# Adaptive LayerNorm with grouped-query attention and a gated MLP: the first eight units' side work in another order, and the last branch marked for prefetch

## The chip, the cores and the metric

The kernel runs on one core of one Trainium2 chip. The metric is the device time of one execution in microseconds (us); a kernel's time is the median of several executions. One further execution is taken by the hardware profiler, and all views of the profile come from that one.

## The reference

`x` is 2048 tokens of 512. There are 32 query heads that share 8 key/value heads of width 128, each with 2048 cached keys. Everything is bfloat16.

```python
mod = (_silu(c) @ w_mod).reshape(...)          # c is 1 x 512, w_mod is 512 x 3072
sa, ca, ga, sb, cb, gb = ...                   # six rows of 512
h = _layernorm(x) * (1 + ca) + sa
x = x + ga * attention(h)                      # q = h @ wq; softmax(q k / sqrt(128)) v; @ wo
h = _layernorm(x) * (1 + cb) + sb
z = gelu(h @ w_in)                             # halves z1, z2 of 896
g = w_sp @ _layernorm(z2) + b_sp
x = x + gb * ((z1 * g) @ w_out)
```

The sum over the 512 rows of `w_mod` may be taken in any order, as long as `c` is taken in the same one.

## The kernel before, in words

**The fast path and the general path.** The kernel computes softmax without subtracting the maximum. It keeps the reciprocals of all softmax sums (`rall`), and checks late in the run that all lie within a safe range; the result is one integer, `flag` (`check_flag`, written in the third stage below). At the very end every engine loads `flag` from on-chip memory into a register (L1360), and `tc.If(redo != 0)` (L1361) runs `general_path`, a whole second kernel that is safe for any input, if the flag is set. On these inputs it is not set, so the program goes past that code. The argument `preferred_fallthrough_block=False` asks that the code for the flag not being set be laid out right behind the branch. L1391 is the end of the whole program, where all engines meet and semaphores are cleared.

**Units and slots.** Attention is a row of 128 units: unit u is key/value head g = u // 16 and the 128 tokens of tile j = u % 16, with its four query heads side by side, so that a score matmul has 512 columns. A unit has 8 slots. In slot i, `qk(u, i)` makes two score matmuls (L922) into a two-bank PSUM tile `s_ps` (two buffers) and one exponential on ScalarE of 128x1024 (L929, `ACTIVATE pT<-s_ps`); `pv(u - 1, i)` makes eight matmuls with the exponentials of the unit before (L944), into `o_ps` (two buffers), and ends every fourth slot with a reciprocal and a scaling on VectorE (L955, L956). So 8 exponentials on ScalarE mark one unit.

**The order by hand.** The schedule is manual: each engine runs its instructions in the order in which the program emits them. Within a slot the loop emits first the entries that `at(unit, slot, fn)` put into `later`, then `qk`, then `pv`, then the entries of `fill`, then (in slots 4 to 7) one matmul of the output projection `wo_proj` (L976) for the unit three back. An instruction on VectorE can therefore hold back everything that was emitted for VectorE after it.

**The side work of the first units.**
- `ln1_stats` (L691, L692 on VectorE, then L672 and L676 on GpSimd) makes mean and reciprocal deviation of up to four token tiles; `ln1_norm` (L680, VectorE) normalises them into `xn`. For the tokens of chunk 0 (512 tokens, of which the first tile is done ahead of everything) and chunk 1, `ln1_turn` (L833) transposes `xn` on TensorE into `misc` (two buffers) and applies scale and shift (L815, VectorE) into `hT`. For chunks 2 and 3, `ln1_dma` (L855) issues four transposing DMAs on SyncE's queue, and `ln1_dma_mod` (L815) applies scale and shift once they have landed.
- `qproj(b, ...)` makes 16 query-projection matmuls (L885), four for each of four heads, into `misc`, and one copy to `qT` on VectorE for each head (L894). Block b serves units 4b to 4b + 3. For block 0 it is done in two parts: 16 small matmuls for the first tile ahead of unit 0, and 16 of 384 columns (`rest_q`) in unit 0, which unit 1 needs.
- `ln1_at(ch, stats, norm, turn)` sets the slots of the three steps of chunk ch. Before: chunk 1 at (0, 7), (1, 3), (1, 6); chunk 2 at (1, 7), (2, 2), (3, 5); chunk 3 at (4, 1), (4, 5), (5, 5). Where the third step is a DMA, it is issued one slot after the second.
- `set_fill(b)`: before, block 1's 16 matmuls are one in each slot of units 2 and 3, and those of block b > 1 one in each of slots 0 to 3 of the four units before block b.
- GpSimd's queue carries, among the reciprocal deviations, four large loads: `wmod_b` (L1083, at (2, 5)), `win_sb` (L1084, at (5, 5)), and `v`, `wo` and `wq` of head 1 (L714, L724, L706, at (5, 3), (6, 3) and (7, 3)). A load waits for its buffer and for its place in that queue, and for nothing else. SyncE's queue carries the transposing DMAs and the load of head 1's keys (L729, at (4, 3)).

**The start.** `c_bf` (L696), one tile of `x` (L697), the first 1024 columns of `w_mod` (`wmod_a`, L698), keys and values are loaded on SyncE's queue. Meanwhile `warm(18)` (L766) runs 18 matmuls on zeros. `mod_columns` (L782) makes scale and shift from `wmod_a`, and the chain through L833, L815, L885 and L894 leads to the first score matmul.

**After attention** come the MLP's first half (L1119, L1158) and four chunks of `spatial` (L1273), each with its output projection (L1294) and the stores to `out` (L1311). The last store is in two halves, one issued by SyncE and one by ScalarE.

Of the kernel before, what the change touches and what calls it, by code (L numbers as in the profile page):

```python
# [15 lines left out]
P = 128  # L16
# [559 lines left out]
def kernel(  # L576
# [23 lines left out]
    REP = HQ // HKV  # L600
# [5 lines left out]
    NDT = D // P  # L606
# [3 lines left out]
    CT = 512 // P  # L610
# [12 lines left out]
    HK = SK // 2  # L623
    k_rows = A_k_cache[0, 0, 0:HK].rearrange("(p t) d -> p t d", p=P)
    v_rows = A_v_cache[0, 0, 0:HK].rearrange("(p t) d -> p t d", p=P)
    wmod_dram = w_mod.rearrange("(dt p) n -> p dt n", p=P)
    c_dram = c[0].rearrange("(j p) -> p j", p=P)
    win_dram = B_w_in.rearrange("(dt p) f -> p dt f", p=P)
    wout_dram = B_w_out.rearrange("(ft p) d -> p ft d", p=P)

# [32 lines left out]
    def bank(name):  # L663
        return psum.tile([P, 512], FP32, name=name)

    def bank2():
        return psum.tile([P, 1024], FP32, name="s_ps")
# [93 lines left out]

    def warm(n):

        w_ps = bank2()
        for k in range(n):
            nc.tensor.matmul(  # L766
                w_ps[:, 0:512].rearrange("p (r d) -> p r d", r=REP),
                lhsT=zeros[:, 0, :],
                rhs=zeros[:],
                start=True,  # L770
                stop=True,
            )
# [23 lines left out]
    def ln1_stats(j0, n):  # L796
        for j in range(j0, j0 + n):
            ln_stats(mv1, j, x_sb[:, j, :])
        return rstd_of(mv1[:, j0 : j0 + n, :], n, "ln1")

    def ln1_norm(j0, n, rstd):
        xns = []
        for j in range(j0, j0 + n):
            xn = res.tile([P, D], BF16, name="xn1", bufs=4)
            normalise(xn[:], x_sb[:, j, :], mv1[:, j, 0:1], rstd[:, j - j0 : j - j0 + 1])
            xns.append(xn)
        return xns

    def hT_of(ch):
        if ch not in hTs:  # L810
            hTs[ch] = res.tile([P, NDT, 512], BF16, name="hT", bufs=NCH)
        return hTs[ch]

    def ln1_mod(dst, src, dt):
        nc.vector.tensor_scalar(  # L815
            out=dst,
            in0=src,
            scalar1=modc[:, NDT + dt : NDT + dt + 1],
            scalar2=modc[:, dt : dt + 1],
            op0=ALU.mult,  # L820
            op1=ALU.add,
        )

    def ln1_turn(j0, n, xns, on_act=()):

        ch, c0 = j0 // CT, (j0 % CT) * P
        hT = hT_of(ch)
        for half in range(2):
            t_ps = bank("misc")[:].bitcast(BF16).rearrange("p (k q) -> p k q", k=2)
            for k in range(2):  # L830
                dt = half * 2 + k
                for jj in range(n):
                    nc.tensor.transpose(  # L833
                        t_ps[:, k, jj * P : (jj + 1) * P],
                        xns[jj][:, dt * P : (dt + 1) * P],
                        ident[:],
                    )
            for k in range(2):
                dt = half * 2 + k
                dst, src = hT[:, dt, c0 : c0 + n * P], t_ps[:, k, 0 : n * P]  # L840
                if dt in on_act:
                    nc.scalar.activation(
                        out=dst,
                        in_=src,
                        func=ACT.Identity,
                        scale=modc[:, NDT + dt : NDT + dt + 1],
                        bias=modc[:, dt : dt + 1],
                    )
                else:
                    ln1_mod(dst, src, dt)  # L850

    def ln1_dma(j0, n, xns):
        hT = hT_of(j0 // CT)
        for jj in range(n):
            nc.sync.dma_start_transpose(out=hT[:, :, jj * P : (jj + 1) * P], in_=xns[jj][:])  # L855

    def ln1_dma_mod(ch):
        for dt in range(NDT):
            ln1_mod(hTs[ch][:, dt, :], hTs[ch][:, dt, :], dt)

    warm(18)
    xns0 = ln1_norm(0, 1, ln1_stats(0, 1))
    mod_columns(0, wmod_a, 0)
# [9 lines left out]
    def qproj(b, heads, c0, n):  # L873

        g, ch = divmod(b, NCH)
        if b not in qTs:
            qTs[b] = early.tile([P, REP, 512], BF16, name="qT")
        one = n * len(heads) <= 512
        ps = {}

        def mm(hh, dt):
            if dt == 0 and (not one or hh == heads[0]):
                ps[0] = bank("misc")
            o0 = (hh - heads[0]) * n if one else 0
            nc.tensor.matmul(  # L885
                ps[0][:, o0 : o0 + n],
                lhsT=wqs[g][:, dt, hh * DH : (hh + 1) * DH],
                rhs=hTs[ch][:, dt, c0 : c0 + n],
                start=(dt == 0),
                stop=(dt == NDT - 1),  # L890
            )
            if dt == NDT - 1 and (not one or hh == heads[-1]):
                hs = heads if one else [hh]
                nc.vector.tensor_copy(  # L894
                    out=qTs[b][:, hs[0] : hs[-1] + 1, c0 : c0 + n],
                    in_=ps[0][:, 0 : len(hs) * n].rearrange("p (h q) -> p h q", q=n),
                )

        return [lambda hh=hh, dt=dt: mm(hh, dt) for hh in heads for dt in range(NDT)]
# [3 lines left out]
    rest0 = {}  # L903
# [7 lines left out]
    def at(it, slot, fn):  # L911
        later.setdefault((it, slot), []).append(fn)
# [142 lines left out]
    def load_wsp(tile_, t, st):  # L1055
        nc.sync.dma_start_transpose(  # L1056
            out=tile_[:, st, :],
            in_=B_w_sp[t * 512 : (t + 1) * 512, st * P : (st + 1) * P],
        )
# [2 lines left out]

    fill = {}
    rest_q = qproj(0, list(range(REP)), P, 512 - P)
    at(0, 3, lambda: ln1_turn(1, CT - 1, rest0["xn"]))
    for k, fn in enumerate(rest_q):
        fill.setdefault((0, 5 + min(k // 5, 2)), []).append(fn)

    def ln1_at(ch, stats, norm, turn):
        st = {}  # L1070
        at(*stats, lambda: st.update(r=ln1_stats(ch * CT, CT)))
        at(*norm, lambda: st.update(x=ln1_norm(ch * CT, CT, st["r"])))
        if ch == 1:
            at(*turn, lambda: ln1_turn(ch * CT, CT, st["x"]))
        else:
            at(norm[0], norm[1] + 1, lambda: ln1_dma(ch * CT, CT, st["x"]))
            at(*turn, lambda: ln1_dma_mod(ch))

    ln1_at(1, (0, 7), (1, 3), (1, 6))
    ln1_at(2, (1, 7), (2, 2), (3, 5))  # L1080
    ln1_at(3, (4, 1), (4, 5), (5, 5))
    rest_w = {}
    at(2, 5, lambda: nc.gpsimd.dma_start(out=wmod_b, in_=wmod_dram[:, :, 2 * D : NMOD]))  # L1083
    at(5, 5, lambda: nc.gpsimd.dma_start(out=win_sb[:], in_=win_dram))  # L1084
# [5 lines left out]
    def set_fill(b):  # L1090

        fs = qproj(b, list(range(REP)), 0, 512)
        for k, fn in enumerate(fs):
            it, slot = ((b - 1) * CT + k // NDT, k % NDT) if b > 1 else (2 + k // 8, k % 8)
            fill.setdefault((it, slot), []).append(fn)

    def wsp0():
# [5 lines left out]
    for g in range(1, HKV):  # L1103
        it = (g - 1) * NT + 4
# [91 lines left out]
    for it in range(NU + 6):  # L1196
        if it < NU:
            if it % CT == 0 and it // CT + 1 < NB:
                set_fill(it // CT + 1)
        elif it == NU:  # L1200
            free_a.close()
            z2p = fast.enter_context(tc.tile_pool(name="z2p", bufs=1))
            zs["z2"] = z2p.tile([P, NT, FH], BF16, name="z2")
# [54 lines left out]
    def check_flag():  # L1258
        f_ps = bank("o_ps")
        nc.tensor.matmul(  # L1260
            f_ps[0:1, 0:1], lhsT=bad[:], rhs=ones_bf[:, 0:1], start=True, stop=True
        )
        nc.vector.tensor_copy(out=flag[:], in_=f_ps[0:1, 0:1])
# [51 lines left out]
    def o2_tile(t, jj):  # L1315
        o2 = bank("o_ps")
        for f in range(NFT):
            o2_mm(o2[:], yTs[t], jj, f)
        finish_tile(t, jj, o2)
# [3 lines left out]
    for t in range(NCH):  # L1323
        yTs[t] = mlp.tile([P, NFT, 512], BF16, name="yT", bufs=2)
        if t == last:
            break
        for f in range(NFT):
            spatial(t, yTs[t], f, 0, 512)
            if t == 1 and f == CT:
                check_flag()  # L1330
            if t > 0 and f < CT:
                o2_tile(t - 1, f)
        if t == 0:
            wsp[last] = wspp.tile([P, NT, 512], BF16, name="wsp")
            for st in range(NT):
                load_wsp(wsp[last], last, st)
    acc = [bank2(), bank2()]
    o2_last = [acc[jj // 2][:, (jj % 2) * 512 : (jj % 2 + 1) * 512] for jj in range(CT)]
    yT = yTs[last]
# [18 lines left out]
    fast.close()  # L1358

    redo = nc.values_load(flag[0:1, 0:1], min_val=0, max_val=P)  # L1360
    with tc.If(redo != 0, preferred_fallthrough_block=False):  # L1361
        general_path(
            tc, A_x, A_k_cache, A_v_cache, A_wq, A_wo, B_x, B_w_in, B_w_sp, B_b_sp, B_w_out,
            c, w_mod, out,
        )
# [30 lines left out]
```

## Time and profile before

| what | us |
|---|---|
| median of 3 runs | 1338.97 (1338.56 to 1339.24) |
| the profiled execution, its own time | 1339.45 |
| its span, first to last instruction | 1337.6 |
| TensorE busy in the span | 1305.1 |
| ScalarE busy in the span | 1079.3 |
| first exponential of unit 0 | 12.40 |
| first exponential of unit 1 | 27.62 |
| first exponential of unit 2 | 37.32 |
| first exponential of unit 4 | 57.02 |
| first exponential of unit 8 | 92.93 |
| last instruction on the data, an output's store, is issued | 1329.39 |

The mean granted TensorE clock over the span is 0.995. In the views, PE is TensorE's matmuls, PEld its weight loads, DVE VectorE, ACT ScalarE, POOL GpSimd, SP SyncE; a q behind the name means the sequencer of that engine. A line of the timeline has its start, its length from first start to last end, the engine, the source line, the operation and its tiles, and in brackets the idle time ahead of it and what ended it.

### The profile page before, as it was taken

How to read it: one execution, taken by the hardware profiler on the slowest of the kernel's cores; microseconds unless marked ns; L12 is line 12 of the kernel's file. 1: busy time of each engine (PE TensorE's matmuls, PEld its weight loads, DVE VectorE, ACT ScalarE, POOL GpSimd, SP SyncE). 2: the span in 40 equal slices, each digit the busy share in tenths (PEclk: the TensorE clock that was granted, in tenths of full speed). 3: DMA queues.
4: the chain of work that ended last, by engine and by line, in shares of the span. 5: the costliest groups of instructions: out<-in, count | busy, mean ns of one | idle time of the engine just before them, and what ended most of it. 6: DMA issues, size and time to landing. Idle time of an engine off the chain costs nothing.

```text
span 1337.6 us, 27647 instructions
## 1 busy us (share of the span) xinstructions
PE 1305.1 (98%) x12126; PEld 859.4 (64%) x12333; DVE 473.1 (35%) x1163; ACT 1079.3 (81%) x1060; POOL 48.6 (4%) x90
## 2 busy tenths in 40 slices
PE   7999999999999999999999999999999999999996
PEld 3666666666666666666666666666666667644444
DVE  4632222222222222222222222222222566783443
ACT  4898999999999999999999999999999999650000
POOL 1200000000000000000000000000000000020000
PEclk8999999999999999999999999999999999999999
DMA  5541022101311121012110310122101111154200
GB/s 158 131 111 17 14 63 37 21 17 33 64 21 21 33 64 21 17 36 65 17 21 17 74 30 14 21 65 36 21 13 21 25 33 33 29 123 82 55 21 27
DMA packets 146368, 57.59 MB, mean 43 GB/s; under 512 B 136544, under 2 KB 141792, under 8 KB 146240
## 3 DMA queue, kind: packets, MB, share of 16 engines
q1 hardware_dynamic: 141888, 39.29, 15.7%
q0 software_dynamic: 4208, 16.39, 4.1%
q8 instruction: 98, 1.61, 0.5%
q14 instruction: 30, 0.25, 0.1%
q10 hardware_dynamic: 144, 0.07, 0.0%
HBM read 21.37 MB, written 2.10 MB: 18 GB/s over the span
## 4 chain that ended last, share of the span: by engine, by line
PE 94%; SPq 2%; DVE 1%; issue 1%; DMA 1%; POOL 0%; ACT 0%; DVEq 0%
PE s_ps L922 35%; PE o_ps L944 35%; PE misc L885 7%; PE misc L976 6%; PE misc L1273 6%; PE s_ps L1119 2%; PE s_ps L1158 2%; SPq L1056 1%; PE o_ps L1294 1%; PE s_ps L1294 0%; DMA wmod_a<-in_w_mod_dram 0%; DMA hT<-xn 0%; DVE bnst L691 0%; DVE qT L894 0%; DMA out_dram<-yout 0%
## 5 line engine op out<-in xcount | busy, mean ns | idle before, releaser
L929 ACT ACTIVATE pT<-s_ps 128x1024 bf16<-128x1024 f32 x1024 | 1045.9, 1024 | 92.2 <-PE s_ps L922 17.1
L944 PEld LDWEIGHTS <-pT 128*128 128x128 bf16 x8192 | 549.3, 98 | 242.4 <-issue 1.8
L944 PE MATMUL o_ps<-v,pT 128*128 128x129 bf16 x8192 | 632.4, 220 | 0.4 <-DVE onorm L956 0.4
L922 PE MATMUL s_ps<-qT,kT 128*128 128x512 bf16 x2048 | 610.6, 380 | 15.5 <-DVE qT L894 4.7
L955 DVE RECIPROCAL rall<-o_ps 128x2 f32<-128x2 f32 x256 | 43.7, 171 | 742.6 <-PE o_ps L944 742.4
L922 PEld LDWEIGHTS <-kT 128*128 128x128 bf16 x2048 | 199.6, 98 | 126.2 <-DVE qT L894 4.8
L885 PE MATMUL misc<-hT,wq_g 128*128 128x512 bf16 (+2 forms) x462 | 167.7, 373 | 0.0
L976 PE MATMUL misc<-wo_g,oT 128*128 128x512 bf16 x388 | 147.0, 379 | 0.0
L956 DVE TENSOR_TENSOR onorm<-o_ps,rall 128x256 bf16<-128x256 f32 x256 | 108.7, 425 | 9.0 <-DVE rall L955 0.3
L1273 PE MATMUL misc<-wsp,z 128*128 128x512 bf16 (+2 forms) x555 | 100.5, 336 | 1.7 <-DVE gb L1288 1.1
L894 DVE CAST qT<-misc 128x512 bf16<-128x512 f32 (+1 forms) x129 | 87.2, 677 | 4.7 <-PE misc L885 4.7
L1273 PEld LDWEIGHTS <-z 128*128 128x128 bf16 x560 | 50.7, 98 | 49.5 <-issue 1.0
L989 DVE TENSOR_TENSOR xacc<-misc,xacc 128x512 f32<-128x512 f32 x112 | 76.2, 680 | 0.0
L885 PEld LDWEIGHTS <-wq_g 128*128 128x128 bf16 x528 | 51.3, 98 | 2.2 <-issue 1.1
L976 PEld LDWEIGHTS <-oT 128*128 128x128 bf16 x512 | 50.1, 98 | 0.7
L1288 DVE TENSOR_TENSOR gb<-misc,bsp_bc 128x512 bf16<-128x512 f32 (+1 forms) x28 | 18.4, 658 | 53.1 <-PE misc L1273 53.1
L712 POOL MEMSET v<- 128x128 bf16 x8 | 1.6, 204 | 715.9 <-issue 606.9
L1119 PE MATMUL s_ps<-win_sb,hT 128*128 128x448 bf16 x128 | 27.0, 352 | 0.1
L1129 ACT ACTIVATE z<-s_ps 128x896 bf16<-128x896 f32 x16 | 14.7, 917 | 14.9 <-PE s_ps L1119 14.9
L1158 PE MATMUL s_ps<-hT,win_sb 128*128 128x512 bf16 x109 | 24.3, 379 | 0.2
L1166 ACT ACTIVATE z1T<-s_ps 128x1024 bf16<-128x1024 f32 x14 | 14.3, 1024 | 10.0 <-PE s_ps L1158 9.1
L691 DVE BATCH_NORM_STATS2 bnst<-x_sb 128x6 f32<-128x512 bf16 x32 | 21.8, 682 | 0.5
(78 smaller groups left out, 281.2 us busy)
## 6 DMA issues: line engine op xcount, KB each, us to landing
v<-in_A_v_cache_dram POOLq DMA_DIRECT2D x7, 512.0 KB, 6.6
wo_g<-in_A_wo_dram POOLq DMA_DIRECT2D x7, 512.0 KB, 4.8
wq_g<-in_A_wq_dram POOLq DMA_DIRECT2D x7, 512.0 KB, 6.0
oT<-onorm SPq DMA_TRANSPOSE x128, 2.4
wsp<-in_w_mod_dram POOLq DMA_DIRECT2D x1, 2048.0 KB, 9.2
out_dram<-yout SPq DMA_DIRECT2D x15, 128.0 KB, 1.7
win_sb<-in_B_w_in_dram POOLq DMA_DIRECT2D x1, 1792.0 KB, 9.8
x_sb<-in_A_x_dram SPq DMA_DIRECT2D x3, 512.0 KB, 5.7
```

Source lines behind the costliest of these rows:

```text
L885: nc.tensor.matmul(ps[0][:, o0 : o0 + n], lhsT=wqs[g][:, dt, hh * DH : (hh + 1) * DH], rhs=hTs[ch][:, dt, c0 : c0 + n], start=(dt == 0), s ...
L894: nc.vector.tensor_copy(out=qTs[b][:, hs[0] : hs[-1] + 1, c0 : c0 + n], in_=ps[0][:, 0 : len(hs) * n].rearrange("p (h q) -> p h q", q=n),)
L922: nc.tensor.matmul(s_ps[:, h * 512 : (h + 1) * 512].rearrange("p (r q) -> p r q", r=REP), lhsT=groups[g]["kT"][:, kt * P : (kt + 1) * P], ...
L929: nc.scalar.activation(out=pTs[u][:, 2 * i : 2 * i + 2, :], in_=s_ps[:].rearrange("p (k q) -> p k q", k=2), func=ACT.Exp, scale=inv_sqrt_dh,)
L944: nc.tensor.matmul(o_ps[:, hh % 2, 0 : DH + 1], lhsT=pTs[u][:, kt, hh * P : (hh + 1) * P], rhs=groups[g]["v1"][:, kt, 0 : DH + 1], start=( ...
L955: nc.vector.reciprocal(out=rall[:, c0 : c0 + 2], in_=o_ps[:, :, DH])
L956: nc.vector.tensor_tensor(out=onorms[u][:, hh - 1 : hh + 1, :], in0=o_ps[:, :, 0:DH], in1=rall[:, c0 : c0 + 2].unsqueeze(2).to_broadcast([ ...
L976: nc.tensor.matmul(X_ps[:], lhsT=oTs[u][:, hh, :], rhs=groups[g]["wo"][:, hh, :], start=(hh == 0), stop=(hh == REP - 1),)
L989: nc.vector.tensor_tensor(out=xaccs[j][:], in0=X_ps[:], in1=xaccs[j][:], op=ALU.add)
L1119: nc.tensor.matmul(ps[0][:, hf * 512 : hf * 512 + FC], lhsT=h2Ts[j // CT][:, dt, (j % CT) * P : (j % CT + 1) * P], rhs=win_sb[:, dt, FH + ...
L1158: nc.tensor.matmul(ps[0][:, k * 512 : (k + 1) * 512], lhsT=win_sb[:, dt, f * P : (f + 1) * P], rhs=h2Ts[2 * ch2 + k][:, dt, :], start=(dt ...
L1273: nc.tensor.matmul(g_ps[:, :n], lhsT=z2[:, st, f * P : (f + 1) * P], rhs=wsp[t][:, st, c0 : c0 + n], start=(st == 0), stop=(st == NT - 1 a ...
```

## The change

Five things change.

1. `c` and `w_mod` are read with another assignment of rows to partitions: partition p gets the neighbouring rows 4p to 4p + 3, where it got rows p, p + 128, p + 256 and p + 384. For `c` this makes one run of 4 elements of each partition, where there were four single elements. It holds for both loads of `w_mod`.
2. `warm` writes to the `o_ps` buffers and no longer to `s_ps`. One warming matmul is added to each of slots 0 to 3 of unit 0.
3. The turn of the rest of chunk 0 moves from slot 3 to slot 4 of unit 0, and `rest_q` is spread 6, 6, 4 over slots 5 to 7, where it was 5, 5, 6.
4. The three steps of chunks 1, 2 and 3 move, and so do the matmuls of blocks 1 and 2. Block 1 is now two to a slot in slots 1 to 7 of unit 2 and slot 0 of unit 3; block 2 is two to a slot in slots 0 to 3 of unit 5 and one to a slot in slots 0 to 3 of units 6 and 7.
5. Ahead of the last chunk of `spatial`, a mark on all engines hints that the branch labelled "redo" is likely taken. The branch gets that label, and the argument for its layout is dropped, so that the layout is chosen automatically.

```diff
-    wmod_dram = w_mod.rearrange("(dt p) n -> p dt n", p=P)
-    c_dram = c[0].rearrange("(j p) -> p j", p=P)
+    wmod_dram = w_mod.rearrange("(p dt) n -> p dt n", p=P)
+    c_dram = c[0].rearrange("(p j) -> p j", p=P)
...
     def warm(n):
 
-        w_ps = bank2()
+        w_ps = bank("o_ps")
         for k in range(n):
             nc.tensor.matmul(
-                w_ps[:, 0:512].rearrange("p (r d) -> p r d", r=REP),
+                w_ps[:].rearrange("p (r d) -> p r d", r=REP),
...
-    at(0, 3, lambda: ln1_turn(1, CT - 1, rest0["xn"]))
+    at(0, 4, lambda: ln1_turn(1, CT - 1, rest0["xn"]))
     for k, fn in enumerate(rest_q):
-        fill.setdefault((0, 5 + min(k // 5, 2)), []).append(fn)
+        fill.setdefault((0, 5 + k // 6), []).append(fn)
+    for i in range(4):
+        fill[0, i] = [lambda: warm(1)]
...
-    ln1_at(1, (0, 7), (1, 3), (1, 6))
-    ln1_at(2, (1, 7), (2, 2), (3, 5))
-    ln1_at(3, (4, 1), (4, 5), (5, 5))
+    ln1_at(1, (1, 0), (1, 5), (1, 7))
+    ln1_at(2, (2, 4), (3, 1), (4, 5))
+    ln1_at(3, (5, 1), (5, 5), (6, 6))
...
         for k, fn in enumerate(fs):
-            it, slot = ((b - 1) * CT + k // NDT, k % NDT) if b > 1 else (2 + k // 8, k % 8)
+            it, slot = (b - 1) * CT + k // NDT, k % NDT
+            if b == 1:
+                it, slot = 2 + (2 + k) // 16, (1 + k // 2) % 8
+            elif b == 2:
+                it, slot = (5, k // 2) if k < 8 else (it, slot)
             fill.setdefault((it, slot), []).append(fn)
...
+    tc.mark_branch_hint_location("redo", "LikelyTaken")
     acc = [bank2(), bank2()]
...
-    with tc.If(redo != 0, preferred_fallthrough_block=False):
+    with tc.If(redo != 0, label="redo"):
```

## The prediction

> **What bounds the kernel now.** I read the page first, then the waits and gaps of TensorE by time, then the first 60 us closely, then the end.
>
> ```profile
> PE 1305.1 (98%) x12126; PEld 859.4 (64%) x12333; DVE 473.1 (35%) x1163; ACT 1079.3 (81%) x1060; POOL 48.6 (4%) x90
> ...
> PE 94%; SPq 2%; DVE 1%; issue 1%; DMA 1%; POOL 0%; ACT 0%; DVEq 0%
> ```
>
> TensorE is busy for 98% of the span and makes 94% of the chain that ended last. So everything between unit 8 and the last store only shifts with the start; the change leaves it alone. What can move is the start, where TensorE waits, and the end, where it is done. The timeline of the start shows the waits:
>
> ```profile
> 15.92 1.38 PE L833 MATMUL misc<-ident,xn 128*128 128x128 bf16 x12 [1.86 <-DVE xn L680]
> ...
> 17.83 1.94 ACT L929 ACTIVATE pT<-s_ps 128x1024 bf16<-128x1024 f32 x2 [2.57 <-PE s_ps L922]
> ...
> 22.73 0.68 DVE L691 BATCH_NORM_STATS2 bnst<-x_sb 128x6 f32<-128x512 bf16 x1
> ...
> 25.93 0.99 DVE L894 CAST qT<-misc 128x384 bf16<-128x384 f32 x2
> ...
> 26.98 0.60 PE L922 MATMUL s_ps<-qT,kT 128*128 128x512 bf16 x2 [3.03 <-DVE qT L894]
> ...
> 27.62 1.02 ACT L929 ACTIVATE pT<-s_ps 128x1024 bf16<-128x1024 f32 x1 [3.58 <-PE s_ps L922]
> ```
>
> The brackets are to be seen. TensorE loses 1.86 us for `xn` ahead of slot 3, and 3.03 us for the last two `qT` casts, which stand in VectorE's order behind four statistics (L691) of a chunk that nobody needs yet. Idle time is paid twice, as the granted clock (PEclk) by windows shows:
>
> ```profile
> 14.13:17.54 3.41, 1.43 (x14) 0.96 (x15) 1.59 (x5) 1.12 (x2) 1.13 (x2) 1.00 1.10 347
> 17.54:20.96 3.42, 3.16 (x9) 1.16 (x8) 1.10 (x3) 2.95 (x3) 0.00 (x0) 0.50 0.59 185
> ...
> 24.37:27.78 3.41, 0.80 (x9) 0.57 (x10) 2.77 (x8) 0.16 (x1) 1.27 (x2) 1.00 0.00 0
> 27.78:31.20 3.42, 3.42 (x24) 2.32 (x22) 1.10 (x4) 2.33 (x3) 0.00 (x0) 0.50 0.01 2
> ```
>
> TensorE was busy for only 1.43 us and 0.80 us of two windows, and ran at half clock in the window after each. At the end, the sequencers' lines of L1361 (the branch) and L1391 (the program's end):
>
> ```profile
> L1361 SPq EVENT_SEMAPHORE  x8: 17/17/17, 1329.1 to 1331.9; - x8
> ...
> L1361 PEldq COMPARE_BRANCH  x2: 90/1858/3627, 1327.8 to 1328.1; - x2
> L1361 SPq COMPARE_BRANCH  x2: 38/48/57, 1329.0 to 1332.2; - x2
> ...
> L1391 SPq EVENT_SEMAPHORE  x14: 17/28/28, 1336.0 to 1337.6; - x14
> ```
>
> SyncE branches twice, at 1329.0 and 1332.2. Between lie its waits for the landing of the stores. After the second it does nothing until 1336.0: 3.7 us, though the branch took 0.04. TensorE's second branch is itself shown with 3.63 us.
>
> [...] here 1.43 us of work was too little, while the window at 10.72 with 1.88 us was enough. [...]
>
> **The change, part by part.** The sum is against the profiled execution, 1339.45 us (span 1337.6); the median of the runs is 0.48 lower.
>
> *Loads of c and w_mod.* TensorE starts its real work when `wmod_a` lands, at 7.39. Its packets have the same size as before. `c` becomes 128 runs where it was 512 elements, ahead of it on the same queue. Its packets ran from 1.8 to 3.1 us, beside the next loads. A gain of 0.4 at most (then `xn`, ready at 6.98, is late instead)[...]. I take zero.
>
> *Unit 0.* The four added matmuls (0.22 us each) fall where TensorE waits for exponentials anyway, so they cost nothing; uncovered, 0.9. Slot 3's scores no longer wait for `xn`. The transposes still start at 15.92 and end near 17.15 (DVE's and GpSimd's order ahead of them is unchanged), followed by slot 4. VectorE's four L815 end at 18.63 as before. From there TensorE has the last of head 0 and all of heads 1 to 3 (13 matmuls of 384 columns, 0.16 us each as 16 of that size take 2.60 at L1273 in the last chunk, 2.1 us) and two pairs of scores (0.43 each): it ends at 21.6, if at full clock. In the window 14.13 to 17.54 it now does one pair more of scores and a warming matmul, some 2.0 us in place of 1.43, above the 1.88 that sufficed; so I take full clock, and 1.1 us more where the window falls badly. The last cast (0.56) follows at once, at 22.3, since chunk 1's statistics are now emitted behind it. Scores take 0.6 more: unit 1's first exponential comes at **22.9, where it was 27.62: 4.7 us**.
>
> *Unit 1.* A slot without side work costs 0.88 us on TensorE (0.43 + 0.45 in the chain) and 0.91 on ScalarE (three exponentials in 2.85 us, the last 1.02). Eight of 0.91 and the 0.8 us of chunk 1's turn make 8.1. Its 16 transposes find `xn`: statistics until 25.6, GpSimd until 26.9, norm until 28.4, slot 7 near 29.3. It took 9.70 (27.62 to 37.32), in part at half clock. **1.5 us.**
>
> *Units 2 and 3.* They took 19.70 (37.32 to 57.02) with 16 query matmuls and 4 output ones, and a wait of 0.89 us for block 1's last cast, which ended just ahead of unit 4. Now: slot 0 at 0.91; seven slots with two query matmuls at 0.88 + 0.44 = 1.32; again 1.32; three at 0.91; four at 1.10: 18.6. The last cast comes seven slots ahead of its user. **1.1 us.** Chunk 2's statistics (3.2 us on VectorE at (2, 4)) delay the casts of heads 1 and 2 behind them; the two `misc` buffers give them until slot 7, four slots of 1.3.
>
> *Units 4 to 7.* 35.9 us against 35.2 busy on TensorE. Transposing DMAs for `hT` took up to 13.2 us to land, those of chunk 3, together with four loads of 3.3 MB from GpSimd's queue, and stalled VectorE by 6.6 and TensorE by 0.38 us. The new slots keep all of it in the same order: the loads still follow chunk 3's deviation, and the DMAs still come four to five slots later. From their issue at (5, 6) to the first TensorE instruction that VectorE's wait can hold, (7, 4), it is as far as from (4, 6) to (6, 4) before. Only head 1's keys are now out of the way. I take zero: a gain of 0.6 if the stall goes, a loss of 0.7 if it doubles. Chunk 2's DMAs meet `wmod_b` as before, and block 2 starts a unit later, so it can wait.
>
> *The end.* With the layout dropped, the general path lies behind the branch, so going past it is one taken branch, at SyncE's 1329.0, ahead of its waits; the second branch is gone. If the hint has the target fetched, SyncE leaves its waits at 1332.3 and goes straight into the closing sequence, which takes 1.6 us. **3.6 us.** If the hint does nothing, the 3.7 us fetch starts at 1329.0 and hides behind the waits until 1331.9: it ends at 1332.7, the semaphores (8 in 0.65 us) at 1333.3, and 2.6 us are still gained. The marks themselves are one sequencer instruction for each engine, between 0.04 and 0.2 us (SEQ_ASSERT 37 ns, FUSED_REGOPS 184 ns at L1360), hidden behind the engines' queued work. Late next are ScalarE and VectorE, whose first end-of-program instruction stood at 1333.2 and 1332.7: just in time.
>
> Sum: 4.7 + 1.5 + 1.1 + 3.6 = 10.9, so 1339.45 becomes 1328.5, and the median 1338.97 becomes **1328.1 us**.
>
> **The rivals.**
> - *A, as worked: 1328.1, 61%.*
> - *B, the hint does not act* [...]: only the overlap helps. 1.0 less: 1329.1, 12%. [...]
> - *C, the branch doesn't change its way*: the automatic layout is the old one, and the last jump stays unhinted. Without the 3.6: 1331.7, 11%.
> - *D, the start has a wait or a slow window more*: half clock in unit 0 (1.1) or a longer hT wait in unit 7 (0.7), up to both: 1329.7, 12%.
> - *E, slower*: [...] 2%.
> - *F, the start's gain is given back at units 2 to 8 by waits of VectorE* behind moved statistics, and C as well: about 1337, 2%.
>
> **How the numbers follow.** The range reaches from all unknowns on the good side (0.4 and 0.6 and half the spread of the runs, below 1328.1: 1326.7; I give 1326.4) over B and D to C: 1331.8. What is left out are E, F and D with C. A measurement of this kernel tells 0.2% (2.7 us) from no change. A to D are all faster by over 7 us; F is within; E is slower: 0.96, 0.02, 0.02.
>
> **What would show it.** Unit 1's first exponential at 22.9 and unit 2's at 31.0; unit 8's near 85.6 (92.93 before); no 0.50 in the clock's windows after the first 4 us; SyncE's COMPARE_BRANCH once, and its closing sequence from about 1325.1 (1332.3 less 7.3), right after the stores' landing. Wrong would be a bracket of over 1 us ahead of L922 in unit 1, or a pause of 3.7 us still behind SyncE's last wait.

## The result, and the profile after

The changed kernel takes 1331.68 us (median of 4 runs, 1329.62 to 1333.13) against 1339.11 us for the kernel before beside it: the ratio is 0.9943, with a 95% interval of 0.9926 to 0.996. That is 7.4 us less. The forecast was 1328.1 us, and 1326.4 to 1331.8 for the range: the time lies at its slow end. The profiled execution took 1333.13 us, with a span of 1331.3, and is the slowest of the four.

The page again begins with TensorE, and a line of the chain shows who now stands in it:

```profile
PE 1316.5 (99%) x12337; PEld 859.9 (65%) x12337; DVE 473.0 (36%) x1163; ACT 1077.1 (81%) x1060; POOL 48.1 (4%) x90
...
PE 96%; SPq 2%; DVE 1%; DMA 1%; issue 0%; POOL 0%; DVEq 0%
```

The timeline of ScalarE alone is the quickest way to see where the start's gain went. Its exponentials (L929) mark the slots; a line joins those that follow without a gap.

```profile
12.51 3.77 ACT L929 ACTIVATE pT<-s_ps 128x1024 bf16<-128x1024 f32 x4 [1.55 <-PE s_ps L922]
17.88 3.06 ACT L929 ACTIVATE pT<-s_ps 128x1024 bf16<-128x1024 f32 x3 [1.60 <-PE s_ps L922]
21.33 1.02 ACT L929 ACTIVATE pT<-s_ps 128x1024 bf16<-128x1024 f32 x1 [0.38 <-PE s_ps L922]
23.24 6.52 ACT L929 ACTIVATE pT<-s_ps 128x1024 bf16<-128x1024 f32 x7 [0.89 <-PE s_ps L922]
...
63.01 18.64 ACT L929 ACTIVATE pT<-s_ps 128x1024 bf16<-128x1024 f32 x17 [0.29 <-PE s_ps L922]
85.42 1.02 ACT L929 ACTIVATE pT<-s_ps 128x1024 bf16<-128x1024 f32 x1 [3.77 <-PE s_ps L922]
87.57 1.02 ACT L929 ACTIVATE pT<-s_ps 128x1024 bf16<-128x1024 f32 x1 [1.12 <-PE s_ps L922]
```

Four exponentials run before ScalarE has to wait in unit 0 (three before), the wait of 3.58 us ahead of unit 1 is now 0.89, and unit 1 begins at 23.24. Then all goes smoothly up to 81.65, where ScalarE waits for 3.77 us, and again for 1.12. Counting eight exponentials to a unit gives this table (us, first exponential of the unit; the last row is the span's end):

| | before | after | less by | forecast |
|---|---|---|---|---|
| unit 0 | 12.40 | 12.51 | -0.11 | 12.40 |
| unit 1 | 27.62 | 23.24 | 4.38 | 22.9 |
| unit 2 | 37.32 | 31.33 | 5.99 | 31.0 |
| unit 4 | 57.02 | 49.80 | 7.22 | 49.6 |
| unit 7 | 84.13 | 76.28 | 7.85 | not given |
| unit 8 | 92.93 | 90.19 | 2.74 | 85.6 |
| last store issued | 1329.39 | 1326.74 | 2.65 | |
| end of the span | 1337.6 | 1331.3 | 6.3 | 1326.7 |

Unit 7 took 13.9 us where its work takes 8.8, and gave 5.1 us back. The waits between 70 and 92 us (who waited for whom, us in total, times, longest) name the cause:

```profile
DVE hT L815 <- DMA hT<-xn: 9.4, 1, 9.4
...
PE o_ps L944 <- DVE onorm L956: 3.1, 1, 3.1
```

In the profile before, the same lines are:

```profile
DVE hT L815 <- DMA hT<-xn: 6.6, 1, 6.6
...
PE o_ps L944 <- DVE onorm L956: 0.4, 1, 0.4
```

VectorE stood for 9.4 us (6.6 before) at the scale of chunk 3, waiting for the transposing DMAs; the scaling L956 stood behind it, and TensorE waited 3.1 us (0.4 before) for that. The clock then took its share, as two windows show (length, busy time of each engine, granted clock, DMA share, GB/s):

```profile
84.76:88.17 3.41, 3.41 (x21) 2.31 (x20) 0.65 (x2) 1.63 (x2) 0.00 (x0) 0.50 0.22 43
88.17:92.00 3.83, 3.83 (x39) 2.53 (x37) 1.84 (x7) 3.23 (x4) 0.00 (x0) 1.00 0.16 32
```

After the wait comes a window at half clock: 21 matmuls in 3.41 us, where the next one has 39 in 3.83. If half of its 3.41 us is lost, that is 1.7 us (an estimate), and with the wait, 3.15 us in the timeline, nearly all of the 5.1.

At the end, the sequencers' lines of the branch (now L1368) and of the program's end (now L1398):

```profile
L1368 SPq EVENT_SEMAPHORE  x8: 17/17/17, 1328.9 to 1329.5; - x8
...
L1368 PEldq COMPARE_BRANCH  x1: 3371/3371/3371, 1325.2 to 1325.2; - x1
L1368 SPq COMPARE_BRANCH  x1: 53/53/53, 1326.3 to 1326.3; - x1
...
L1398 SPq EVENT_SEMAPHORE  x14: 17/28/173, 1329.5 to 1331.2; - x14
```

SyncE branches once, at 1326.3, pauses for 2.6 us, finds the stores landed, and walks through its eight semaphores and the closing sequence; the only wait left there is 0.2 us for ScalarE, which branches at 1327.7 and has its own pause until 1330.3. From the last store's issue to the end it is 4.6 us (1326.74 to 1331.3), where it was 8.2 (1329.39 to 1337.6): 3.65 less. But TensorE's one branch still takes 3.4 us. So nothing shows a target that was brought early, and no engine shows an instruction of the line of the mark (L1343).

### The profile page after: what moved, and what is told of

It is laid out like the page before. It is cut to its first block, busy times and chain, and to the rows that moved or that the text cites. A ratio compares the mean times of both kernels' runs of the same rounds, so it can differ in the third digit from the quotient of the medians.

```text
span 1331.3 us, 27856 instructions
## 1 busy us (share of the span) xinstructions
PE 1316.5 (99%) x12337; PEld 859.9 (65%) x12337; DVE 473.0 (36%) x1163; ACT 1077.1 (81%) x1060; POOL 48.1 (4%) x90
## 3 DMA queue, kind: packets, MB, share of 16 engines
q8 instruction: 98, 1.61, 0.5%
## 4 chain that ended last, share of the span: by engine, by line
PE 96%; SPq 2%; DVE 1%; DMA 1%; issue 0%; POOL 0%; DVEq 0%
PE o_ps L944 35%; PE s_ps L922 33%; PE misc L976 8%; PE misc L885 8%; PE misc L1279 6%; PE s_ps L1125 2%; PE s_ps L1164 2%; SPq L1056 1%; PE o_ps L1300 1%; PE o_ps L766 1%; PE s_ps L1300 0%; DMA hT<-xn 0%; SPq L855 0%; PE misc L833 0%; DMA out_dram<-yout 0%
## 5 line engine op out<-in xcount | busy, mean ns | idle before, releaser
L929 ACT ACTIVATE pT<-s_ps 128x1024 bf16<-128x1024 f32 x1024 | 1043.6, 1024 | 91.6 <-PE s_ps L922 16.9
L944 PEld LDWEIGHTS <-pT 128*128 128x128 bf16 x8192 | 549.3, 98 | 245.0 <-issue 4.3
L944 PE MATMUL o_ps<-v,pT 128*128 128x129 bf16 x8192 | 632.3, 220 | 3.1 <-DVE onorm L956 3.1
L976 PE MATMUL misc<-wo_g,oT 128*128 128x512 bf16 x512 | 194.3, 379 | 0.0
L885 PE MATMUL misc<-hT,wq_g 128*128 128x512 bf16 (+2 forms) x528 | 190.3, 373 | 0.0
L956 DVE TENSOR_TENSOR onorm<-o_ps,rall 128x256 bf16<-128x256 f32 x256 | 108.6, 424 | 9.0 <-DVE rall L955 0.3
L1279 PE MATMUL misc<-wsp,z 128*128 128x512 bf16 (+2 forms) x560 | 100.7, 336 | 1.1 <-DVE gb L1294 1.1
L1279 PEld LDWEIGHTS <-z 128*128 128x128 bf16 x560 | 50.7, 98 | 49.6 <-issue 1.1
L1135 ACT ACTIVATE z<-s_ps 128x896 bf16<-128x896 f32 x16 | 14.7, 917 | 14.9 <-PE s_ps L1125 14.9
```

The source lines that it names most:

```text
L885: nc.tensor.matmul(ps[0][:, o0 : o0 + n], lhsT=wqs[g][:, dt, hh * DH : (hh + 1) * DH], rhs=hTs[ch][:, dt, c0 : c0 + n], start=(dt == 0), s ...
L929: nc.scalar.activation(out=pTs[u][:, 2 * i : 2 * i + 2, :], in_=s_ps[:].rearrange("p (k q) -> p k q", k=2), func=ACT.Exp, scale=inv_sqrt_dh,)
L944: nc.tensor.matmul(o_ps[:, hh % 2, 0 : DH + 1], lhsT=pTs[u][:, kt, hh * P : (hh + 1) * P], rhs=groups[g]["v1"][:, kt, 0 : DH + 1], start=( ...
L956: nc.vector.tensor_tensor(out=onorms[u][:, hh - 1 : hh + 1, :], in0=o_ps[:, :, 0:DH], in1=rall[:, c0 : c0 + 2].unsqueeze(2).to_broadcast([ ...
L976: nc.tensor.matmul(X_ps[:], lhsT=oTs[u][:, hh, :], rhs=groups[g]["wo"][:, hh, :], start=(hh == 0), stop=(hh == REP - 1),)
L1279: nc.tensor.matmul(g_ps[:, :n], lhsT=z2[:, st, f * P : (f + 1) * P], rhs=wsp[t][:, st, c0 : c0 + n], start=(st == 0), stop=(st == NT - 1 a ...
```

## The experiments

The theory was: the end's gain comes from the layout alone, and the mark does nothing; the start gains 7.85 us up to unit 7, of which unit 7 gives up to 5 back, since chunk 3's transposing DMAs are held up by the loads from GpSimd's queue, and VectorE's order passes their lateness on to TensorE. The rivals: the hint acts; the transposing DMAs are slow by themselves. Kernels of one group ran on one chip beside the same runs of the kernel before, which took 1340.05 us in the first group (no_mark, old_end, end_only, win_late), 1340.15 in the second (scale_late, loads_early, stats_only, no_warm) and 1339.05 in the third (the runs whose names begin with le). So times of different groups may differ by about 1 us for that reason alone.

### The mark alone: no_mark

```diff
-    tc.mark_branch_hint_location("redo", "LikelyTaken")
```

> The changed kernel without the prefetch mark; all else stays. Theory (the mark does nothing; the end's gain comes from the layout of the branch alone): no change, 1331.7 us, within the spread that the changed kernel showed (1329.6 to 1333.1), SyncE's fetch behind its one branch still 2.6 us and TensorE's still 3.4. Rival (the hint brings the target block early): over 1 us slower than the changed kernel and longer fetches.

It took 1330.52 us (1329.45 to 1332.13), ratio 0.9928 (0.9914 to 0.9941). Instruction by instruction, this program and the changed one are the same on all five engines: used in this way, the mark emits nothing. So this run is also a second sample of the changed kernel, and shows how far unit 7 varies: in its profile the wait is 1.60 us, without half clock, and unit 7 takes 10.7 us. SyncE pauses for 2.6 us and TensorE for 3.35 again.

### The end alone, taken away and added: old_end and end_only

```diff
 # old_end: the changed kernel with
-    tc.mark_branch_hint_location("redo", "LikelyTaken")
...
-    with tc.If(redo != 0, label="redo"):
+    with tc.If(redo != 0, preferred_fallthrough_block=False):
 # end_only: the kernel before with
+    tc.mark_branch_hint_location("redo", "LikelyTaken")
...
-    with tc.If(redo != 0, preferred_fallthrough_block=False):
+    with tc.If(redo != 0, label="redo"):
```

> The changed kernel with the branch at the end as it was before: no mark, no label, the code for the unset flag next. Theory (the new layout is worth the 3.65 us by which the time from the last store to the end shrank): 1335.3 us. Rival (the end's gain is not the layout's, or the start's new timing made it): 1331.7.

> The kernel before with the new end alone (mark, label, automatic layout). Theory: 3.65 us less than before, 1335.4, and the same two branches become one on SyncE. Rival (both parts only work together): 1339.1.

With the old end the changed kernel took 1334.21 us (1332.56 to 1335.51), ratio 0.9953 (0.9939 to 0.9966): 3.7 us more than without the mark, in the same group. The kernel before with the new end took 1336.39 us (1334.46 to 1338.03), ratio 0.9973 (0.9962 to 0.9983): 3.7 us less than before. The two agree, so the layout is worth 3.7 us with either start. The sequencers' lines of the branch in the profile with the old end show both branches again:

```profile
L1367 SPq EVENT_SEMAPHORE  x8: 17/17/17, 1323.9 to 1326.8; - x8
...
L1367 SPq COMPARE_BRANCH  x2: 38/48/57, 1323.8 to 1327.2; - x2
```

and its line of the program's end has the pause behind the second, from 1327.2 to 1330.9:

```profile
L1397 SPq EVENT_SEMAPHORE  x14: 17/28/28, 1330.9 to 1332.5; - x14
```

In the old layout the waits for the stores come first, and the pause of 3.7 us after them; in the new one the pause of 2.6 us runs while the stores land. That the pause is a fetch of instructions is the author's reading and not shown by these lines. Beside it, the DMA queue named "instruction" q8 has a packet at 1326.2 in the changed kernel's profile, 1.0 us after TensorE's branch, and one at 1329.1 in the profile before, 1.0 us after TensorE's second; whose fetch a packet is isn't named there. Why SyncE's pause is 2.6 us in one layout and 3.7 in the other was not tested.

### Less traffic beside chunk 3: win_late

```diff
-    at(5, 5, lambda: nc.gpsimd.dma_start(out=win_sb[:], in_=win_dram))
+    at(22, 5, lambda: nc.gpsimd.dma_start(out=win_sb[:], in_=win_dram))
```

> The changed kernel with the 1.8 MB load of win_sb moved from (5, 5) to (22, 5), behind a load on GpSimd's queue that waits. Theory (chunk 3's transposing DMAs land late because they share the DMA engines with 3.3 MB from GpSimd's queue): they land some 5 us sooner, VectorE's wait of 9.4 us at L815 falls below 4, the 3.15 us wait in unit 7 and the half clock behind it go, and the time is about 1327.0 us with less spread between runs. Rival (the transposing DMAs are slow by themselves): wait and time stay, 1331.7.

It took 1328.64 us (1328.29 to 1330.9), ratio 0.9914 (0.9901 to 0.9928), 1.9 us less than the run without the mark. Unit 7 takes 8.81 us; TensorE's wait there is gone. The profiled execution is nevertheless the slowest of the five (1330.9 us), and for another reason: near 1244 us TensorE waits 1.96 us at L1279, in `spatial`, for VectorE, which has waited 8.4 us for the first chunk's stores, and the clock is half from 1245.87 to 1249.28. So the spread of the changed kernel's runs need not come from unit 7 alone. The theory's direction held, its size not: VectorE still waits 5.5 us at L815 (below 4 was expected), and the first of the DMAs lands 12.0 us after its issue. The time from issue to landing of the last load on GpSimd's queue (`wq`) and of chunk 3's first DMA, both added to their issue, says why:

| kernel | `wq` issued + to landing | first `hT` DMA issued + to landing |
|---|---|---|
| before | 64.35 + 11.8 = 76.2 | 62.97 + 13.2 = 76.2 |
| after | 65.82 + 14.4 = 80.2 | 64.43 + 16.1 = 80.5 |
| no_mark | 65.84 + 13.2 = 79.0 | 64.45 + 14.6 = 79.0 |
| win_late | 65.36 + 11.4 = 76.8 | 64.72 + 12.0 = 76.7 |

In all four, the transposing DMA that was issued first lands when the last load lands; the profiles of old_end, end_only, scale_late, no_warm and stats_only agree within 0.25 us. So it isn't enough to take the largest load away.

### The wait at another place: scale_late

```diff
-    ln1_at(3, (5, 1), (5, 5), (6, 6))
+    ln1_at(3, (5, 1), (5, 5), (7, 6))
```

> The changed kernel with chunk 3's scale and shift (L815) at (7, 6) in place of (6, 6); no transfer moves. Theory (the late landing costs only because VectorE's queue stands at L815 while scalings that TensorE needs wait behind it): the transposing DMAs still land 14 to 16 us after the first issue, but VectorE's wait at L815 is under 2 us, the wait in unit 7 goes, and the time is that of the run with the late win_sb load, about 1328.6 us. Rival (block 3 needs hT at once, or the DMA itself holds TensorE): 1330.5 or more.

It took 1329.35 us (1328.82 to 1331.2), ratio 0.9924 (0.9911 to 0.9938). The DMAs are as late as ever (up to 14.9 us), VectorE doesn't wait for them at all, and unit 7 takes 9.1 us in the profile. So the lateness by itself costs little: it costs where VectorE's order lets other work stand behind it. Two of the five runs are at 1331.1 and 1331.2; which wait they met was not profiled. The wait near 1244 us is still in this kernel (1.33 us in its profile), and win_late shows what it can cost.

### No traffic beside chunk 3: loads_early

```diff
-    at(5, 5, lambda: nc.gpsimd.dma_start(out=win_sb[:], in_=win_dram))
+    at(22, 5, lambda: nc.gpsimd.dma_start(out=win_sb[:], in_=win_dram))
...
         at(it, 3, lambda g=g: load_k(g))
+        if g == 1:
+            at(it, 4, lambda: load_v(1, nc.sync))
+            at(it, 5, lambda: load_wo(1, nc.sync))
+            at(it, 6, lambda: load_wq(1, nc.sync))
+            continue
...
-            (nc.sync, nc.scalar)[k].dma_start(out=out_dram[:, j, s], in_=yout[:, s])
+            (nc.scalar if t == 0 else (nc.sync, nc.scalar)[k]).dma_start(out=out_dram[:, j, s], in_=yout[:, s])
```

> The changed kernel with win_sb's load at (22, 5), the loads of v, wo and wq of head 1 on SyncE's queue at (4, 4) to (4, 6), right behind head 1's keys, and the stores of the first token chunk issued by ScalarE. Theory: with no load left beside them, chunk 3's four transposing DMAs land within 8 us of the first issue, VectorE's wait at L815 falls below 1 us, and unit 7 takes 8.8; and TensorE's wait of 1 to 2 us near 1244, where the first chunk's stores stand behind 16 transposing DMAs on SyncE's queue, goes too: about 1326.8 us. Rival (the transposing DMAs are slow by themselves; the wait near 1244 has another cause): 1328.6.

It took 1326.83 us, ratio 0.9899 (0.9884 to 0.9914), and its four runs lie between 1326.68 and 1326.92. The view of the tile `hT` between 40 and 95 us shows the landing (least, median, most), here for chunks 2 and 3 together (chunk 2's still meet the load of `wmod_b`, from 40.66 to 50.71 us):

```profile
DMA to landing us min/median/max: 2.4/4.0/8.0
```

Between 62 and 95 us, for chunk 3 alone, the same view gives 2.4, 2.5 and 4.1 us. The waits between 62 and 92 us no longer hold one for `hT`, nor one of TensorE:

```profile
POOL ve_ln L672 <- DVE mv L692: 20.0, 1, 20.0
DVE rall L955 <- PE o_ps L944: 16.0, 6, 3.2
ACT pT L929 <- PE s_ps L922: 0.6, 2, 0.3
```

VectorE's remaining wait is for TensorE (L944), as it should be where TensorE is the bound. The kernel holds a second edit, to be read apart: with the first chunk's stores issued by ScalarE, TensorE's wait near 1244 us (1.59 us in the profile without the mark, 1.15 in the changed kernel's) is gone as well. Of the 3.7 us between this run and the one without the mark (each beside some 1340.1 us for the kernel before), the two edits take some 1.9 (unit 7: 10.7 less 8.8) and 1.6. That second part is the difference that is left, about what the wait near 1244 took; it was not taken apart by a run of its own. This version beats both kernels.

### The parts of the start: stats_only, no_warm, le_no_warm, le_old_rows, le_turn3

stats_only is the kernel before with one edit:

```diff
-    ln1_at(1, (0, 7), (1, 3), (1, 6))
+    ln1_at(1, (1, 0), (1, 5), (1, 7))
```

> The kernel before with one edit: chunk 1's steps at (1, 0), (1, 5), (1, 7) as in the changed one. Theory (the 3.03 us wait ahead of unit 1 and the half clock in unit 1 come from the four statistics ahead of the last casts): unit 1 starts 3.0 us sooner, unit 1 takes 8.1 us in place of 9.7, so about 4.6 us less than before, 1335.4. Rival (xn and slot 3's turn set unit 0's end, the statistics only fill): under 1.5 us less, 1338.6 or more.

It took 1336.14 us (1335.36 to 1337.31), ratio 0.9972 (0.996 to 0.9983): 4.0 us less. In its profile unit 1 begins at 24.57 (3.05 sooner) and takes 8.10 us (1.6 less), which is what was expected, but the first number is met in part by luck. TensorE still waits 1.85 us for `xn` ahead of slot 3, and yet the half clock that followed this wait before (17.54 to 20.96) is not there. Counted from `xn` (L680, at 15.45 before, 15.82 here), head 1's cast, which stands ahead of the statistics in both kernels, starts 1.05 us sooner. That much goes with the clock; the order of the statistics has some 2.4 (3.05 and the 0.37 by which `xn` is late, less 1.05). Unit 3 gives 1.0 back (11.87 us for 10.89), with block 1's projections still where they were: its last cast now stands behind a wait of 3.7 us at L815, and TensorE waits 1.9 us for it. So the statistics' gain is kept whole only with the other moves.

no_warm is the changed kernel without the four warming matmuls, le_no_warm the same edit in the version with the early loads:

```diff
-    for i in range(4):
-        fill[0, i] = [lambda: warm(1)]
```

> The changed kernel without the four warming matmuls in slots 0 to 3 of unit 0. Theory [...]: where the window falls badly, unit 0's last slots run at half clock and unit 1 starts some 1.1 us later; median 1330.5 to 1331.6 us, with a 0.50 window between 14 and 24 us in the profile. Rival (enough work is there without them): 1330.5, no such window.

> The version with the early loads, whose runs lie within 0.24 us of each other (1326.83 us), without the four warming matmuls. Theory [...]: within 0.3 us, 1326.8, perhaps a single run 1 us longer. Rival (they buy full clock in unit 0): 1 us more, 1327.9.

no_warm took 1329.94 us (1329.6 to 1333.98), ratio 0.993 (0.9916 to 0.9943), no more than with them, and its profile has no half clock in unit 0; unit 7's own spread covers what they may do. On the steadier base there is more to see: le_no_warm took 1326.99, 1326.89, 1328.33 and 1328.62 us (ratio 0.9913, 0.9898 to 0.9928). Two runs are as fast as le_old_rows (1326.95 us, in the same group and with the matmuls), two are 1.4 to 1.7 us longer, with a mean clock of 0.998 for 0.999. So the matmuls don't gain in every run, but may keep a slow window away. The profiled run was a fast one, and that the window is unit 0's was not seen. It could be: in this profile the 3.41 us from 12.96 hold only 1.42 us of TensorE's work, and in the one of loads_early no 3.41 us of unit 0 hold less than 2.14.

le_old_rows is the version with the early loads, with `(dt p)` and `(j p)` again for `w_mod` and `c`:

> The version with the early loads and the old assignment of rows for c and w_mod. Theory (wmod_a's landing sets the start, and it has the same packets either way): c lands 1 us later, xn 1 us later, but TensorE's first matmul on wmod_a moves by less than 0.3 us: 1326.8 us. Rival (the 512 single elements hold wmod_a up): 0.4 us more or over, 1327.2.

It took 1326.95 us (1326.68 to 1327.13), ratio 0.9905 (0.989 to 0.992): no difference that these runs show (loads_early, in another group, took 1326.83). VectorE gets `c` at 3.51, where it gets it at 2.5 with the new rows. TensorE waits for `wmod_a` until 7.70; with the new rows it does so until 7.61 in le_no_warm. (In loads_early its first matmul on `wmod_a` starts at 7.75, but behind warming matmuls that ended late, so that start says nothing of the landing.)

le_turn3 is the version with the early loads, with chunk 0's turn back at slot 3:

```diff
-    at(0, 4, lambda: ln1_turn(1, CT - 1, rest0["xn"]))
+    at(0, 3, lambda: ln1_turn(1, CT - 1, rest0["xn"]))
```

> The version with the early loads and chunk 0's turn back at slot 3 of unit 0. Theory (slot 3's scores again wait for xn, ScalarE starts its fourth exponential 2.6 us later, but TensorE's chain from xn through the projections to the last cast is what ends unit 0, so that only one pair of scores, 0.43 us, and what ScalarE then holds back is added): unit 1 starts 0.4 to 0.9 us later, 1327.2 to 1327.7. Rival (ScalarE's eight exponentials end unit 0): 1.3 us or more, 1328.1.

It took 1328.98 us (1328.13 to 1329.1), ratio 0.9919 (0.9906 to 0.9933): 2.0 us more than le_old_rows in the same group. That is more than the theory allowed. It is within the rival's "or more", but not by the rival's cause: unit 1's first scores wait for the cast of `qT` (0.65 us), not for ScalarE. The windows of its profile (columns as above) say what was left out:

```profile
12.50:16.57 4.07, 2.08 (x10) 0.67 (x7) 2.66 (x8) 2.85 (x3) 1.12 (x2) 1.00 1.11 305
16.57:19.98 3.41, 3.32 (x17) 1.85 (x17) 1.73 (x5) 1.02 (x1) 0.00 (x0) 0.50 0.93 291
```

With slot 3 behind the turn, TensorE waits 1.64 us for `xn`, is busy for 2.08 of 4.07 us, and gets half clock for the next 3.41 us; unit 1 begins at 25.30, 1.9 us later than with the turn at slot 4. The pair of scores ahead of the wait is worth 0.43 us as work; the rest, some 1.5 us, goes with the clock (half of 3.41 us would be 1.7).

Whether half clock followed a wait went also with where the wait fell. In the profiles before and after, each fall to half clock lies a whole number of stretches of 3.413 us after the first full clock: 4, 7 and 389 of them after 3.89 us in the one, 23 and 387 after 6.25 us in the other. The moment of the first full clock differs (these two, where the warming matmuls shorten from 0.63 to 0.38 us, and 4.84 us in stats_only's profile). Here are five waits of TensorE, each with the emptiest window of this kind that it touches and TensorE's busy time there (us):

| kernel | wait of TensorE | window | busy | next window |
|---|---|---|---|---|
| before | 1.86 | 14.13 to 17.54 | 1.43 | half clock |
| le_turn3 | 1.64 | 13.16 to 16.57 | 1.43 | half clock |
| win_late | 1.96 | 1242.46 to 1245.87 | 1.45 | half clock |
| stats_only | 1.85 | 11.66 to 15.07 | 1.61 | full clock |
| old_end | 2.19 | 1242.71 to 1246.13 | 1.70 | full clock |

The longest of the five has no half clock behind it. In the profiles before and after, the windows with up to 1.43 us of work were each followed by half clock, and none with 1.88 us or more was; the 1.61 and 1.70 us of the table, with full clock behind them, lie between. So le_turn3's 2.0 us hold for this placement; its fifth run, at 1328.13, was 0.85 us shorter and was not profiled.

## Why the prediction came out as it did

- **Loads of c and w_mod, zero:** right. le_old_rows shows none. What little the profile has (0.11 us later) goes with the first warming matmuls, which, by their length (0.63 us, then 0.38), ran at half clock up to 6.25 us after the start, and up to 3.89 in the profile before: TensorE comes from them to `wmod_a` without a wait.
- **Unit 0 (4.7), unit 1 (1.5), units 2 and 3 (1.1):** right, with 4.38, 1.60 and 1.23, as was full clock after the first microseconds, until 84.8. The most of it is the order of VectorE's queue: stats_only alone has 3.05 and 1.6 of it, though some 1.05 of the 3.05 is full clock that fell to it by the window's place. The warming matmuls "cost nothing": the fast runs of le_no_warm (1326.89 and 1326.99 us) are no faster than le_old_rows, which has them; that they save 1.5 us in some runs is suggested, not shown.
- **Units 4 to 7 (zero, at worst a loss of 0.7):** this step failed, and nearly all of the miss is here. Units 4 to 6 went a little better than forecast (26.5 us for 27.1). Then the stall didn't go, stay at 0.38 or double: it became 3.15 us, and with the half clock behind it cost 5.1 us in the profiled execution; in the one without the mark it was 1.60 and cost 1.9. The step reasoned from slots: as many slots from issue to need as before, hence as much slack. It took the landing time, 13.2 us in one execution, for a constant. It was 16.1 us and 14.6 us in two profiles of the same program. And it left out what the prediction itself had read from the windows at the start: a wait of TensorE can be paid a second time by the clock. Rival D has the right wait, in unit 7, but with half clock in unit 0 and not behind that wait; its "up to both" (1.1 and 0.7 make 1.8, hence 1329.9 and not the 1329.7 given) is about what no_mark's profile shows and less than half of the 5.1.
- **The end (3.6):** right in size, 3.65, by luck, and wrong in how. Of the two ways given, the hint was taken to act; it isn't in the program at all. Rival B's mechanism is the true one, and its price was the mis-sized term: the pause, which the author took for a fetch, was put at 3.7 us as behind SyncE's second branch, but SyncE's pause behind the one branch is 2.6 us and ends just as the stores have landed, so that B loses nothing against A. No run here shows what the pause is made of, or a hint at work.
- **Marks on the queues (0.04 to 0.2 us, hidden):** there are none.
- **Rivals C, E and F:** C is excluded by the one branch in the profile and by old_end, E (slower by the mark) has nothing to act by, and of F a part came: a wait of VectorE in units 2 to 8 gave back 5.1 us, but behind the late DMAs and not behind the moved statistics, and without C.

The sum of the steps, 10.9, was 6.3 in the profiled execution and 9.5 in the group of no_mark (1340.05 less 1330.52). That the time still lies within the range owes something to the luck at the end: with the 2.6 us that the prediction gave to a hint that does nothing, it would have been some 1332.7 us, beyond the range. What is open: why the first transposing DMA took 14.6 us in one execution and 16.1 in another, though it and the loads were issued within 0.03 us of the same times. That the two queues share the DMA engines was the author's cause for the late landings; how their transfers delay each other was not tested.

## What to carry to other kernels

Where each engine runs in a fixed order, ask of every wait on a slow transfer what stands behind it in the queue, and give a transfer that runs beside bulk loads a landing time with a spread (13.2, 14.6 and 16.1 us in three profiles here), not the one that a single trace shows; moving the bulk loads away, with the stores' move beside it, took the spread of the runs from 3.5 us (1329.62 to 1333.13) to 0.24. A wait of some 1.6 us or more on TensorE should be priced as a chance of a slow clock window as well, by the work that is left in any 3.41 us around it: half clock followed a wait of 1.64 us in le_turn3, with 1.43 us of work in its window, and none followed one of 1.60 us in no_mark. And where a program branches past a large unused block, look at what the pause behind the branch runs beside: here the layout in which it ran beside the landing of the last stores was 3.7 us shorter.

## What the runs showed that was not expected

- A transposing DMA on SyncE's queue that was issued among loads on GpSimd's queue landed with the last of them: 76.2 and 76.2, 80.2 and 80.5, 79.0 and 79.0, 76.8 and 76.7 us in four profiles. With no loads beside them (chunk 3 in loads_early), the longest of four took 4.1 us.
- A hint mark with a label on the branch left every engine's instructions as they are.
- A window of 3.41 us with 1.43 us of matmuls in it, 42% busy, was followed by half clock for the next 3.41 us (before and le_turn3), and the same wait for `xn`, where the windows fell otherwise (1.61 us in the emptiest, stats_only), was not.
